# Linear attention with a spatial gating MLP on one core: separate key and query units instead of one unit per head pair

## The chip, the cores and the metric

The kernel runs on one NeuronCore of a Trainium2 chip, in one launch. The metric is the device time of a run in microseconds, as the median of repeated runs. A profile of one execution shows what each engine did: PE is TensorE, ACT is ScalarE, DVE is VectorE, POOL is GpSimd, SP is the engine that only issues DMAs here.

## The reference

Batch 8, 8 heads, 576 tokens, head size 64, 128 features. What is computed, cut to what matters:

```python
def phi(x):
    proj = einsum('bhsd,df->bhsf', x, w_phi)
    proj = proj - max(abs(proj), axis=-1, keepdims=True)
    return concatenate([exp(proj), exp(-proj)], axis=-1)      # 256 features
q_p, k_p = phi(q), phi(k)
kv = einsum('bhsf,bhsd->bhfd', k_p, v);  z = sum(k_p, axis=2)
attn = einsum('bhsf,bhfd->bhsd', q_p, kv) / (einsum('bhsf,bhf->bhs', q_p, z)[..., None] + 1e-06)

x = attn of a batch as (576 tokens, 512)                      # all heads of a token side by side
h = maximum(x @ w_in, 0);  u, v = halves of h                 # 512 columns each
v_n = (v - mean(v)) / sqrt(var(v) + 1e-06)                    # over the 512 columns
v_s = einsum('ts,bsd->btd', w_spatial, v_n) + b_spatial[None, :, None]
out = (u * v_s) @ w_out
```

So `kv` and `z` of a batch need all 576 keys of that batch, a query only needs `kv`; the second half (called B here) needs all heads of a token for `u` and `v`, and all tokens of a batch for the spatial product.

## The kernel before, in words

A batch's 576 tokens are cut into 512 main tokens, four blocks (`NB`) of 128, and 64 tail tokens. The tails of two batches (a group `g`) share one tile of 128 rows.

**Units.** The attention half (A) is cut into 36 units. A main unit is a head pair `pj` of a batch `b`, and holds the keys *and* the queries of all 512 tokens of two heads; a tail unit holds keys and queries of all heads of the two tails of a group. Each unit passes through stages, each in a function:

- `a_transpose` puts k and q with the head dimension on the partitions: with PE and a copy in the first two batches, afterwards `cross` has done it with a DMA transpose on SP's queue (`kT_b`, `qT_b`).
- `a_keys` multiplies by `w_phi` (`by_token`, L232, a 128x256 matmul each, two heads at once with a block-diagonal `wphi2`), takes the largest absolute value on DVE (L244, `mk`) and the two exponentials on ACT (L247, `kf`). `a_scale` scales v by exp of that maximum on POOL (L272, `vs`); the tail's is `tail_scale` (`vst`).
- `a_queries` does the same up to the maximum (L258, `mq`), which POOL splits into a high and a low part (`mhl`); `a_max_t` transposes that on PE (`mT`).
- `a_qfeat` forms the projections with features on the partitions (L304) and subtracts the maxima by one more matmul per head (L308, with `sel`), then two exponentials on ACT (L321, `qf`).
- `a_kv` sums over the keys (L334, L336 for the tail's keys). `a_num` multiplies `qf` by `kv` (L354) and divides in `norm` on DVE (`x`). `a_x_t` transposes `x` to `xT`: on PE with a DVE copy for the first nine units and the last four, otherwise by a DMA transpose on SP's queue (L363).

**The B half.** Its work is a list of tasks of some 0.85 us of matmuls each: `b_v` (L403; then Relu on ACT, statistics on DVE), `b_ln` (POOL: four small operations in `root`, then `normalize`, which writes `vn`), `b_u` (L456), `b_s` (the spatial product, L477 with four `vn` blocks and L478 with the tail's `vnt`; then times `u` on DVE), `b_o` (L500, a copy on ACT, a store on SP), and their tail versions. `b_tasks(b)` gives all tasks of a batch in one go when the last head pair's `xT` has been issued, since a token of `xT` is complete only then. For an odd batch the order is tail `v`, four `v`, `b_ln`, four `u`, tail `u`, the spatial tasks of the even batch, those of the odd batch, then the outputs of both. Batches 0 and 1 (`SPLIT`) are each finished alone.

**The order.** `step(i)` writes down, for each stage in `ORDER`, the unit that is due (`LAGS`: sums two steps after the keys, attention three, out four), and after each stage `fill(share)` takes tasks off the front of the B queue as far as a credit allows, which grows by `RATE` times share, at most to `CAP`. The queue is first in, first out. Loads are put at fixed steps ahead of their unit (`AT`, `AB`, `XP`): k, q and their tails and all weights on POOL's queue, with a cast to bf16 on the way; v, the stores and the DMA transposes on SP's. A tile framework then places semaphores and may move an instruction past others that are not pinned to program order. [...]

Of the kernel before, what the change touches and what calls it, by code (L numbers as in the profile page):

```python
# [11 lines left out]
ALU = mybir.AluOpType  # L12
# [4 lines left out]
def kernel(  # L17
# [29 lines left out]
    POS = [0, 2, 1, 3]  # L47
# [28 lines left out]
    def alloc(b):  # L76
        st[b] = dict(
            q=ld.tile([P, H, NB * D], BF16, tag="q_bf", name="q_bf", bufs=2),
            k=ld.tile([P, H, NB * D], BF16, tag="k_bf", name="k_bf", bufs=2),
            v=ld.tile([P, H * NB, D], FP32, tag="v_f", name="v_f"),  # L80
        )

    def alloc_tail(g):
        gs[g] = dict(
            q=ld.tile([P, H, D], BF16, tag="q_tl", name="q_tl", bufs=1),
            k=ld.tile([P, H, D], BF16, tag="k_tl", name="k_tl", bufs=1),
            v=ld.tile([P, H, D], FP32, tag="v_tl", name="v_tl", bufs=1),
        )

    def load(x, b, h0=0, n=H):  # L90
        if b not in st:
            alloc(b)
        pin(nc.gpsimd.dma_start)(out=st[b][x][:, h0:h0 + n], in_=main_ap(q if x == "q" else k, b, h0, n))

    def load_v(b, eng):
        pin(eng.dma_start)(out=st[b]["v"].rearrange("p (h c) d -> p h (c d)", h=H), in_=main_ap(v, b))

    def load_tail(x, g):
        if g not in gs:
            alloc_tail(g)  # L100
        t, eng = dict(q=(q, nc.gpsimd), k=(k, nc.gpsimd), v=(v, nc.sync))[x]
        for i in range(2):
            pin(eng.dma_start)(out=gs[g][x][i * TL:(i + 1) * TL], in_=tail_ap(t, 2 * g + i))

    def cross(b):
        d = st[b]
        for x in ("k", "q"):
            d[x + "T"] = ld.tile([P, 2 * H, P], BF16, tag=x + "T_b", name=x + "T_b", bufs=2)
            pin(nc.sync.dma_start_transpose)(out=d[x + "T"], in_=d[x].rearrange("p h x -> p (h x)"))


    wphi_f = cpool.tile([P, F], FP32)
    for i in range(2):
        nc.scalar.dma_start(out=wphi_f[i * D:(i + 1) * D, :], in_=w_phi)
    alloc(0)
    first = {}
    for x, t in (("k", k), ("q", q)):
        first[x] = s2.tile([P, 2, NB * D], FP32, tag="ob", name="first", bufs=4)
        pin(nc.sync.dma_start)(out=first[x], in_=main_ap(t, 0, 0, 2))
    ident = cpool.tile([P, P], BF16)  # L120
    make_identity(nc, ident)
    zero = cpool.tile([P, 1], BF16)
    pin(nc.vector.memset)(zero, 0.0)
    wphi2 = cpool.tile([P, 2 * F], BF16)
    pin(nc.vector.memset)(wphi2, 0.0)
    neghalf = cpool.tile([P, NB + 1], FP32)
    pin(nc.vector.memset)(neghalf, -0.5)

    w_spT = cpool.tile([P, NB + 2, S], BF16)
    pin(nc.vector.memset)(w_spT[:, NB:NB + 2, :], 0.0)  # L130
# [3 lines left out]
    for i in range(NM):  # L134
        for tiles, name in ((mhl, "mhl"), (mT, "mT")):
# [6 lines left out]
    pin(nc.vector.tensor_tensor)(out=sel1, in0=ident[:, 0:H], in1=ident[:, H:2 * H], op=ALU.add)  # L142
    pin(nc.vector.tensor_scalar)(out=sel, in0=sel1.unsqueeze(2).to_broadcast([P, H, F]), scalar1=-1.0,
                                 scalar2=None, op0=ALU.mult)
    for x in ("k", "q"):
        pin(nc.vector.tensor_copy)(out=st[0][x][:, 0:2], in_=first[x])
    vst, vnt = [], []
    for i in range(2):
        t = cpool.tile([P, 2, 2, H, DA], BF16, name=f"vst{i}")
        pin(nc.scalar.copy)(out=t.rearrange("p b s h d -> p (b s h d)"), in_=zero.to_broadcast([P, 4 * H * DA]))  # L150
        vst.append(t)
        if i == 0:
            for y in range(2):
                r = slice(y * D, (y + 1) * D)
                pin(nc.scalar.copy)(out=wphi2[r, y * F:(y + 1) * F], in_=wphi_f[r, :])
        t = cpool.tile([P, 2, HALF], BF16, name=f"vnt{i}")
        for bl, row in ((0, TL), (1, 0)):
            pin(nc.scalar.copy)(out=t[:, bl, :], in_=ident[:, row:row + 1].to_broadcast([P, HALF]))
        vnt.append(t)
    load_v(0, nc.sync)  # L160
    for x in ("k", "q", "v"):
        load_tail(x, 0)
    load("k", 0, 2, 2)
    load("q", 0, 2, 2)
    load("k", 0, 4, 4)
    load("q", 0, 4, 4)

# [6 lines left out]
    nc.sync.dma_start(out=bsp_row[TL:TL + 1, :], in_=moe_b_spatial)  # L174
    nc.sync.dma_start(out=bsp_row[0:1, :], in_=moe_b_spatial)
# [9 lines left out]
    EK = 7  # L185
    def transpose_spatial(i):

        pt = psum.tile([P, S], BF16, tag="bank", name="pt")
        if i < NB:
            sc = POS[i]  # L190
            for tp, c in enumerate(POS):
                nc.tensor.transpose(out=pt[:, tp * P:(tp + 1) * P], in_=wsp[:, c, bass.ds(sc, P, step=NB)],
                                    identity=ident)
            nc.tensor.transpose(out=pt[:, T0:S], in_=wspt[:, bass.ds(sc, P, step=NB)],
                                identity=ident[:TL, :TL])
            nc.vector.tensor_copy(out=w_spT[:, i, :], in_=pt)
            return
        for bl in range(2):
            lo = bl * TL
            for tp, c in enumerate(POS):  # L200
                nc.tensor.transpose(out=pt[lo:lo + TL, tp * P:(tp + 1) * P], in_=wspr[:, c, :], identity=ident)
            nc.tensor.transpose(out=pt[lo:lo + TL, T0:S], in_=wspt[:, T0:S], identity=ident[:TL, :TL])
            nc.vector.tensor_copy(out=w_spT[lo:lo + TL, NB + bl, :], in_=pt[lo:lo + TL, :])
        for bl, row in ((0, TL), (1, 0)):
            r = slice(row, row + 1)
            pin(nc.scalar.copy)(
                out=w_spT[r, NB + bl, 0:T0].rearrange("o (a b p) -> o a b p", a=2, b=2),
                in_=bsp_row[r, 0:T0].rearrange("o (p b a) -> o a b p", a=2, b=2))
# [3 lines left out]
    def a_transpose(u):  # L212
        src = st[u["b"]] if u["pair"] else gs[u["g"]]
        if "kT" in src:
            for x in ("kT", "qT"):
                u[x] = src[x][:, 4 * u["pj"]:4 * u["pj"] + 4, :] if u["pair"] else src[x]
            return
        for x, copy in (("k", nc.vector.tensor_copy if u["i"] < EK else nc.scalar.copy), ("q", nc.vector.tensor_copy)):
            pt = psum.tile([P, 4, P], BF16, tag="bank", name="pt")
            for j in range(4):  # L220
                if u["pair"]:
                    blk = src[x][:, 2 * u["pj"] + j // 2, (j % 2) * P:(j % 2 + 1) * P]
                else:
                    blk = src[x][:, 2 * j:2 * j + 2, :]
                nc.tensor.transpose(out=pt[:, j, :], in_=blk, identity=ident)
            u[x + "T"] = a1.tile([P, 4, P], BF16, tag=x + "T", name=x + "T", bufs=2 if x == "k" else 4)
            copy(out=u[x + "T"], in_=pt)
# [7 lines left out]

    def a_keys(u):

        u["mk"] = small.tile([P, H], FP32, tag="mk", name="mk")
        u["kf"] = feat.tile([P, 2, H, F], BF16, tag="kf" if u["pair"] else "kf_t", name="kf",
                            bufs=4 if u["pair"] else 2)  # L240
        for half in range(2):
# [4 lines left out]
            for s, sc in ((0, 1.0), (1, -1.0)):  # L246
                nc.scalar.activation(out=u["kf"][:, s, hs, :], in_=pk, func=AF.Exp, bias=0.0, scale=sc)  # L247

    def a_queries(u):

        m, early = mhl[u["i"] % NM], u["i"] < EARLY
        if not early:
            mq = small.tile([P, H], FP32, tag="mq", name="mq")
        for half in range(2):
            pq = by_token(u["qT"], half)
            if early and half == 0:
                mq = pq[:, 0, 0:H]
            nc.vector.tensor_reduce(out=mq[:, 4 * half:4 * half + 4], in_=pq, axis=AX.X, op=ALU.max,  # L258
                                    apply_absolute_value=True)
        eng = nc.vector if early else nc.gpsimd  # L260
# [3 lines left out]
    def a_scale(u):  # L264
        em = small.tile([P, 2, H], FP32, tag="em" if u["pair"] else "em_t", name="em", bufs=3 if u["pair"] else 1)
        for s, sc in ((0, -1.0), (1, 1.0)):
            nc.scalar.activation(out=em[:, s, :], in_=u["mk"], func=AF.Exp, bias=0.0, scale=sc)  # L267
        if u["pair"]:
            pj = u["pj"]
            vs = feat.tile([P, 2, H, DA], BF16, tag="vs", name="vs", bufs=4)  # L270
# [5 lines left out]
        else:  # L276
            d = gs[u["g"]]
            d["vs"], d["unit"], d["em"] = vst[u["g"] % 2], u, em
            for bl in range(2 if u["i"] > 1 else 1):
                tail_scale(u["g"], bl)  # L280
# [15 lines left out]
    def a_qfeat(u):  # L296
# [3 lines left out]
        for half in range(2):  # L300
            pq = psum.tile([P, 4, P], FP32, tag="bank", name="pq")
            if u["pair"]:
                for par in range(2):
                    nc.tensor.matmul(out=pq[:, 2 * par:2 * par + 2, :], lhsT=wphi2[:, par * F:(par + 1) * F],  # L304
                                     rhs=u["qT"][:, 2 * half:2 * half + 2, :], start=True, stop=False)
                    for x in range(2):
                        j = 4 * half + 2 * x + par
                        nc.tensor.matmul(out=pq[:, 2 * par + x, :], lhsT=sel[:, j, :], rhs=m,  # L308
                                         start=False, stop=(x == 1))
            else:  # L310
                for x in range(4):
                    h = 4 * half + x
                    nc.tensor.matmul(out=pq[:, x, :], lhsT=wphi2[:, (h % 2) * F:(h % 2 + 1) * F],
                                     rhs=u["qT"][:, h // 2, :], start=True, stop=False)
# [369 lines left out]
```

## Time and profile before

| what | value |
|---|---|
| median of 3 runs | 291.54 us (287.78 to 293.93) |
| span of the profiled execution, first to last instruction | 286.4 us |
| PE busy | 261.6 us, 91% |
| ACT busy | 229.3 us, 80% |
| DVE busy | 201.8 us, 70% |
| POOL busy | 182.2 us, 64% |
| moved by DMA | 40.31 MB, mean 141 GB/s |

The page gives no time of its own for the profiled execution but the span; the runs lie 1.4 to 7.5 us above it. In a row of busy tenths each digit is a fortieth of the span, 7.2 us here. In a timeline a line is a start, a duration, an engine, a source line, an operation, what is written and read, and a count; several instructions of one kind that overlap are one line, and in brackets stands the idle time before them and what ended it. In the sums by stretch each engine has its busy time and, in brackets, its count of instructions, in the order PE, PE's weight loads, DVE, ACT, POOL; then come PE's clock, the DMA share and GB/s.

### The profile page before, as it was taken

How to read it: one execution, taken by the hardware profiler on the slowest of the kernel's cores; microseconds unless marked ns; L12 is line 12 of the kernel's file. 1: busy time of each engine (PE TensorE's matmuls, PEld its weight loads, DVE VectorE, ACT ScalarE, POOL GpSimd, SP SyncE). 2: the span in 40 equal slices, each digit the busy share in tenths (PEclk: the TensorE clock that was granted, in tenths of full speed). 3: DMA queues.
4: the chain of work that ended last, by engine and by line, in shares of the span. 5: the costliest groups of instructions: out<-in, count | busy, mean ns of one | idle time of the engine just before them, and what ended most of it. 6: DMA issues, size and time to landing. Idle time of an engine off the chain costs nothing.

```text
span 286.4 us, 7965 instructions
## 1 busy us (share of the span) xinstructions
PE 261.6 (91%) x3070; PEld 178.6 (62%) x3070; DVE 201.8 (70%) x509; ACT 229.3 (80%) x517; POOL 182.2 (64%) x320
## 2 busy tenths in 40 slices
PE   1378889999999999999989999999999999999983
PEld 1157776777666776767557687666667676545441
DVE  4389997977958877598696887578688864354610
ACT  4949998899799988999998679799999746566033
POOL 8159998798336899479689954835969600058200
PEclk9999999999999999999999999999999999999999
DMA  6989999976568499999955994999111003500037
GB/s 185 203 171 120 206 219 223 163 203 71 79 147 186 102 187 155 173 245 196 130 94 102 225 191 87 264 287 255 32 22 32 7 2 122 211 3 0 0 90 242
DMA packets 81706, 40.31 MB, mean 141 GB/s; under 512 B 50242, under 2 KB 77058, under 8 KB 81668
## 3 DMA queue, kind: packets, MB, share of 16 engines
q1 hardware_dynamic: 54180, 28.32, 43.0%
q0 software_dynamic: 27328, 11.41, 35.5%
q8 instruction: 24, 0.39, 0.6%
q14 instruction: 14, 0.11, 0.2%
q10 hardware_dynamic: 160, 0.07, 0.1%
HBM read 32.85 MB, written 9.44 MB: 148 GB/s over the span
## 4 chain that ended last, share of the span: by engine, by line
PE 61%; ACT 14%; DVE 11%; DMA 9%; POOL 2%; issue 2%; ACTq 0%; SPq 0%; POOLq 0%; DVEq 0%
PE pv L403 10%; PE ps L477 8%; PE po L500 7%; PE pu L456 7%; PE ps L232 5%; ACT qf L321 5%; ACT kf L247 5%; PE pv L334 4%; DMA q_tl<-in_q_dram 4%; PE pn L354 4%; DMA out_dram<-ob 3%; PE pq L308 3%; PE pq L304 3%; DVE mk L244 3%; PE ps L478 2%; DVE mq L258 2%
## 5 line engine op out<-in xcount | busy, mean ns | idle before, releaser
L247 ACT ACTIVATE kf<-ps 128x512 bf16<-128x512 f32 x144 | 77.7, 692 | 5.6 <-DVE mk L244 5.4
L272 POOL TENSOR_TENSOR vs<-v_f,em 128x512 bf16<-128x512 f32 x64 | 65.6, 1049 | 23.6 <-ACT em L267 22.6
L321 ACT ACTIVATE qf<-pq 128x512 bf16<-128x512 f32 x128 | 68.2, 675 | 8.5 <-PE pq L308 8.5
L244 DVE TENSOR_REDUCE mk<-ps 128x4 f32<-128x512 f32 x72 | 46.1, 677 | 2.5 <-PE ps L232 2.0
L258 DVE TENSOR_REDUCE mq<-ps 128x4 f32<-128x512 f32 x62 | 39.9, 681 | 4.2 <-PE ps L232 3.4
L502 ACT COPY ob<-po 128x512 f32<-128x512 f32 (+1 forms) x37 | 21.6, 610 | 19.9 <-PE po L500 16.2
L406 DVE BATCH_NORM_STATS2 stats<-vr 128x6 f32<-128x512 bf16 (+1 forms) x37 | 24.8, 687 | 15.8 <-ACT vr L405 15.7
L477 PE MATMUL ps<-w_spT,vn 128*128 128x512 bf16 x128 | 32.8, 379 | 0.0
L456 PE MATMUL pu<-xT,w_in_bf 128*128 128x512 bf16 x128 | 31.6, 379 | 0.0
L403 PE MATMUL pv<-w_in_bf,xT 128*128 128x512 bf16 x128 | 31.2, 379 | 0.0
L480 DVE TENSOR_TENSOR uT<-ps,uT 128x512 bf16<-128x512 f32 x32 | 22.0, 689 | 12.7 <-PE ps L478 11.5
L500 PE MATMUL po<-w_out_bf,uT 128*128 128x512 bf16 x128 | 30.4, 379 | 0.0
L308 PE MATMUL pq<-mT,sel 128*128 128x128 bf16 x256 | 30.0, 219 | 0.0
L308 PEld LDWEIGHTS <-sel 128*128 128x128 bf16 x256 | 25.1, 98 | 3.9
L405 ACT ACTIVATE vr<-pv 128x512 bf16<-128x512 f32 (+1 forms) x37 | 23.3, 691 | 4.0 <-PE pv L403 3.9
L354 PEld LDWEIGHTS <-qf 128*128 128x128 bf16 x512 | 20.4, 97 | 8.2 <-issue 1.7
L345 DVE TENSOR_TENSOR x<-pn,rc 128x256 bf16<-128x256 f32 x64 | 25.0, 418 | 0.5
L420 POOL TENSOR_SCALAR vn<-vr,rs 128x512 bf16<-128x512 bf16 x32 | 24.3, 773 | 0.8
L334 PE MATMUL pv<-vs,kf 128*128 128x66 bf16 x512 | 24.5, 194 | 0.2 <-ACT kf L247 0.2
L354 PE MATMUL pn<-kv,qf 128*128 128x66 bf16 x512 | 22.3, 193 | 1.3 <-ACT qf L321 1.2
L334 PEld LDWEIGHTS <-kf 128*128 128x128 bf16 x512 | 21.7, 97 | 1.8 <-issue 0.9
L304 PE MATMUL pq<-qT_b,wphi 128*128 128x256 bf16 x96 | 22.4, 273 | 0.0
(120 smaller groups left out, 530.8 us busy)
## 6 DMA issues: line engine op xcount, KB each, us to landing
v_f<-in_v_dram SPq DMA_DIRECT2D x8, 1024.0 KB, 10.7
out_dram<-ob SPq DMA_DIRECT2D x32, 256.0 KB, 3.6
k_bf<-in_k_dram POOLq DMA_DIRECT2D x7, 512.0 KB, 7.0
q_bf<-in_q_dram POOLq DMA_DIRECT2D x7, 512.0 KB, 8.7
v_tl<-in_v_dram SPq DMA_DIRECT2D x8, 128.0 KB, 7.7
w_in_bf<-in_moe_w_in_dram POOLq DMA_DIRECT2D x2, 512.0 KB, 8.7
out_dram<-ob SPq DMA_DIRECT2D x8, 128.0 KB, 2.4
k_tl<-in_k_dram POOLq DMA_DIRECT2D x8, 64.0 KB, 6.8
```

The lines of the kernel that those rows point to most:

```text
L244: nc.vector.tensor_reduce(out=u["mk"][:, hs], in_=pk, axis=AX.X, op=ALU.max, apply_absolute_value=True)
L247: nc.scalar.activation(out=u["kf"][:, s, hs, :], in_=pk, func=AF.Exp, bias=0.0, scale=sc)
L258: nc.vector.tensor_reduce(out=mq[:, 4 * half:4 * half + 4], in_=pq, axis=AX.X, op=ALU.max, apply_absolute_value=True)
L272: nc.gpsimd.tensor_tensor(out=vs[:, s, :, 0:D], in0=st[u["b"]]["v"][:, pj * H:(pj + 1) * H, :], in1=em[:, s, :].unsqueeze(2).to_broadcast( ...
L308: nc.tensor.matmul(out=pq[:, 2 * par + x, :], lhsT=sel[:, j, :], rhs=m, start=False, stop=(x == 1))
L321: nc.scalar.activation(out=qf[:, s], in_=pq, func=AF.Exp, bias=0.0, scale=sc)
L334: nc.tensor.matmul(out=pv[:, hh, s, :], lhsT=u["kf"][:, s, 4 * hh + c, :], rhs=u["vs"][:, s, 4 * hh + c, :], start=(c == 0), stop=False)
L354: nc.tensor.matmul(out=pn[:, pos, :], lhsT=u["qf"][hh][:, s, pos, :], rhs=d["kv"][:, 2 * u["pj"] + hh, s, :], start=(s == 0), stop=(s == 1))
L403: nc.tensor.matmul(out=pv[r], lhsT=lhs(kc), rhs=w_in_bf[:, kc, HALF:DFF], start=(kc == 0), stop=(kc == KC - 1))
L456: nc.tensor.matmul(out=pu, lhsT=w_in_bf[:, kc, dc * P:(dc + 1) * P], rhs=d["xT"][:, kc, :], start=(kc == 0), stop=(kc == KC - 1))
L477: nc.tensor.matmul(out=ps, lhsT=d["vn"][:, sp, cs], rhs=w_spT[:, sp, 0:T0], start=(sp == 0), stop=False)
L500: nc.tensor.matmul(out=po[r], lhsT=lhs(dc), rhs=w_out_bf[:, dc, :], start=(dc == 0), stop=(dc == KC - 1))
```

## The change

Keys and queries become units of their own. A key unit is a head pair of a batch as before, without queries; a query unit is a block `c` of 128 tokens with all eight heads. Tails are key units and query units too. Since a query unit holds all heads of its tokens, its `x` and `xT` are complete by themselves: `a_x_t` issues one DMA transpose per block, and `add_tasks` puts the block's `b_v` into the B queue at once; the rest of the batch follows at the last block. Five key units (batch 0 and the tail of group 0) lead, then query units and key units alternate, so the keys of a batch run beside the queries of the batch before. There are 72 half-sized units, so the rate of B tasks per step falls from 3.12 to 1.9, and the credit shares are spread evenly.

Smaller parts: by-token projections of queries are eight 128x128 matmuls a unit (`q_by_token`), the projection with features on the partitions is one 128x512 matmul per half (`a_qfeat`); `u` of batch 0 is made block by block (`u_block`); blocks are no longer held in the order 0, 2, 1, 3 (`POS`); the tail is never split by batch; fills of `vst` and `vnt` move from ACT to DVE and into the loop; `w_phi` is loaded by POOL's queue straight into `wphi2` with a cast; the first q is no longer loaded through SP; `q` of batch 0 comes in one load behind the k loads. `kf`, `vs`, `qf` and `kv` get one more buffer or so. PE transposes of `x` are left for query units 0 to 8 and the last two.

```diff
+    first = s2.tile([P, 2, NB * D], FP32, tag="ob", name="first", bufs=4)
+    pin(nc.sync.dma_start)(out=first, in_=main_ap(k, 0, 0, 2))
...
+    for i in range(2):
+        pin(nc.gpsimd.dma_start)(out=wphi2[i * D:(i + 1) * D, i * F:(i + 1) * F], in_=w_phi)
+    load_v(0)
+    load("k", 0, 2, 2)
+    load("k", 0, 4, 4)
+    load_tail("k", 0)
+    load_tail("v", 0)
+    load("q", 0)
+    load_tail("q", 0)
...
     def a_x_t(u):
+        if u["main"]:
+            d = st[u["b"]]
+            if u["c"] == 0:
+                d["xT"] = s2.tile([P, NB, KC, P], BF16, tag="xT", name="xT", bufs=3)
+            dst = d["xT"][:, u["c"]]
+            if XX <= u["i"] < NQ - 2:
+                nc.sync.dma_start_transpose(out=dst, in_=u["x"].rearrange("p h d -> p (h d)"))
+                return
...
+    ks, qs = [], []
     for g in range(G):
-        if g > 0:
-            units.append(dict(pair=False, g=g, i=len(units)))
...
+        pair = k_main(2 * g) + k_main(2 * g + 1)
+        ks += pair[:NP] + [tail_unit("k", g)] + pair[NP:] if g == 0 else [tail_unit("k", g)] + pair
+        qs += q_main(2 * g) + [tail_unit("q", g)] + q_main(2 * g + 1)
...
+    LEAD = 5
+    units = ks[:LEAD]
+    for i in range(NQ):
+        units.append(qs[i])
+        if i + LEAD < len(ks):
+            units.append(ks[i + LEAD])
...
+        u["step"] = dict(next=i - 1, keys=i, sums=i + 2) if u["kind"] == "k" else dict(
+            next=i - 1, queries=i, maxima=i + 1, features=i + 2, attention=i + 3, out=i + 4)
...
+    def add_tasks(u):
+        g = u["g"]
+        if not u["main"]:
+            queue.append((MM, lambda: b_v_tail(g)))
+            queue.append((MM, lambda: b_u_tail(g)))
+            add_spatial(2 * g)
+            return
+        b, c = u["b"], u["c"]
+        queue.append((MM, lambda: b_v(b, c)))
...
+        if c < NB - 1:
+            return
+        queue.append((0.0, lambda: b_ln(b)))
...
+            queue.extend((MM, lambda dc=dc: b_u(b, dc)) for dc in range(KC))
+        if b % 2 == 1:
+            queue.extend((MS, lambda dc=dc: b_s(b, dc)) for dc in range(KC))
+            queue.append((MS, lambda: b_s_tail(g)))
+            queue.append((MM, lambda: b_o_tail(g)))
+            queue.extend((MM, lambda j=j: b_o(b, j)) for j in range(NB))
...
-    ORDER = (("keys", 0.375), ("queries", 0.25), ("attention", 0), ("sums", 0.25),
-             ("next", 0.125), ("features", 0), ("out", 0), ("maxima", 0))
-    RATE = 3.12
+    ORDER = (("keys", 0.2), ("queries", 0.2), ("features", 0.2), ("attention", 0.2), ("sums", 0.2),
+             ("next", 0), ("out", 0), ("maxima", 0))
+    RATE = 1.9
     CAP = 2.11
```

## The prediction, made before the changed kernel was run

> **What bounds the kernel now.** I read, in this order, the busy rows of the page, the sums by stretch, the timeline for the price of each matmul width, and the tile view of `xT`. The busy rows first:
>
> ```profile
> PE 261.6 (91%) x3070; PEld 178.6 (62%) x3070; DVE 201.8 (70%) x509; ACT 229.3 (80%) x517; POOL 182.2 (64%) x320
> ...
> PE   1378889999999999999989999999999999999983
> PEld 1157776777666776767557687666667676545441
> DVE  4389997977958877598696887578688864354610
> ```
>
> PE is the engine that is nearly always busy, except in the first eight slices (57 us), where DVE shows nines instead. The sums by stretch (0 to 60, 60 to 270, 270 to the end) put numbers on that:
>
> ```profile
> 0.00:60.00 60.00, 43.88 (x546) 33.33 (x547) 47.69 (x136) 48.06 (x106) 46.73 (x78) 1.00 1.17 187
> 60.00:270.00 210.00, 206.59 (x2442) 139.76 (x2441) 151.36 (x369) 175.92 (x404) 135.44 (x243) 1.00 0.71 127
> 270.00:287.00 17.00, 11.18 (x86) 5.49 (x84) 2.76 (x4) 5.27 (x9) 0.00 (x0) 0.99 0.43 140
> ```
>
> The first busy column is PE. From 60 to 270 us it idles 3.4 us of 210; at the end 5.2 (286.4 - 270 - 11.2). A busy PE need not be one that streams, so I price the streams from the timeline:
>
> ```profile
> 38.17 0.66 PE L354 MATMUL pn<-kv,qf 128*128 128x66 bf16 x16 [0.16 <-ACT qf L321]
> 41.24 0.60 PE L232 MATMUL ps<-wphi,kT 128*128 128x256 bf16 x4
> ...
> 262.38 1.06 PE L468 MATMUL pu<-xTt,w_in_bf 128*128 128x128 bf16 x16
> 274.97 7.07 PE L500 MATMUL po<-w_out_bf,uT 128*128 128x512 bf16 x32
> ```
>
> Less one matmul's own duration (0.19, 0.27, 0.22, 0.38 us, from the groups) and divided by the count less one: 0.032, 0.109, 0.056 and 0.216 us for widths 66, 256, 128, 512; width 64 I take at 0.029. The program has 584 matmuls of 512, 416 of 256, 584 of 128, 1280 of 66, 206 of 64: 126.1 + 45.3 + 32.7 + 41.0 + 6.0 = 251.1 us. The span is 286.4, so 35.3 us is lost: 3.4 in the middle, 5.2 at the end, hence 26.7 in the first 60 us. The kernel is a PE stream that is full after the start; only the start offers anything large.
>
> **What the Trainium skill says.** "TensorE: Matmul & The Clock Gate", section "Step-by-step: what each phase is for": matmuls stay in program order, only weight loads are pulled ahead. So one matmul that waits stops all PE work behind it. The trace agrees: PE's gap of 3.35 us before the `k_tl` transposes (12.9 us) is followed by nothing from other streams. The same page's section "The HAM clock gate" has a half-rate clock when PE is sparse: four 256-wide matmuls take 1.06 us at 18.8 us and 0.60 at 23.7, so this start pays it although the clock row reads 9. [...] The tile view of `xT` shows the spread:
>
> ```profile
> DMA to landing us min/median/max: 2.4/3.9/7.7
> ```
>
> **The change, part by part.**
>
> *Matmul work.* The new order has 624 of 512, 176 of 256, 884 of 128, 1280 of 66, 166 of 64: 134.8 + 19.2 + 49.5 + 41.0 + 4.8 = 249.3 us. By-token queries become 128 wide (256 of them), feature projections become 512 wide, batch 0's `u` becomes 128 wide. Gain 1.8 us. ACT loses 18 instructions (fills, `kT` copies), POOL 3, DVE gains one: same loads, ACT still some 205 us if a 512-wide eviction is 0.48 (four `qf` from 23.20 to the next `kf` at 25.13), below PE. Buffers only grow.
>
> *Start.* Key work of batch 0 goes first, with five key units before a query. Loads are reordered: `w_phi` now goes through POOL's queue, then k, k tail, q, q tail, with v on SP. The bytes up to the last of them are the same, and before they landed by 22.0 us; I expect q at about 22. Five key units need DVE 5 x 1.5 and ACT 5 x 2.1 = 10.6 us, so they cannot fill the time up to 22; no B work exists then. k of batch 1 is issued on POOL behind two `vs` groups (2.3 us each) that wait for v (before: landed 12.4, now sharing with k, perhaps 14), so issued near 19 to 20; 7 us to landing gives about 27, against 28.4 before. Its four PE transposes stand between the `sums` of batch 0, so all PE waits there. From then to the first spatial matmul DVE owns the rate. Work there: five key units at 1.5 and one at 1.2, five query units at 3.0 (two reductions 1.2, `qB` 0.33 to 0.66, norms 0.86, small copies), two more half done at 1.9, B work 6.3, `kv` 1.4, the fills that moved from ACT and from before the loop 2.5: 38 us. First spatial matmul at 27 + 38 = 65 at full DVE, 67 with a 5% loss; the order has 37.4 us of matmul work ahead of it, so the start loses about 29.6 against 26.7: +3. Bounds: -4 (q and k land 5 us earlier, DVE still limits) to +9.
>
> *Middle: the `xT` transposes lose their cover.* Before, tasks of a batch were queued in one go behind a long queue; `v` came long after the last DMA transpose. Now each block's `v` is queued as it is out, at a rate of 1.9 a step, and followed step by step in the code that queue is empty, or nearly, at the last block of batches 2 to 6. There `v` follows its own transpose in the same step. Between the end of that block's attention matmuls and its `v` the order leaves 3.7 us of matmuls in five places (last block of 2, 4, 6; third block of 3 and 5) and 2.0 in two (last block of 3 and 5). The way from attention to `xT`: drain and norms 0.8, DVE queue 0.5, transpose 3.9 (median): 5.2 us. PE stands 1.5 us in five places and 3.2 in two: 14 us. Bounds from 2.4 to 7.7 us per DMA: 2 and 38. What waits behind `v`: all PE, then ACT and DVE with it.
>
> *Middle: normalisation loses its cover.* The chain of batch 7's LN in the timeline:
>
> ```profile
> 259.18 0.60 ACT L405 ACTIVATE vr<-pv 128x512 bf16<-128x512 f32 x1 [0.27 <-PE pv L403]
> ...
> 260.53 0.18 DVE L407 BATCH_NORM_AGGREGATE mv<-stats 128x2 f32<-128x6 f32 x1
> ...
> 261.87 0.23 POOL L413 TENSOR_SCALAR var<-mv 128x4 f32<-128x4 f32 x1
> ...
> 263.94 3.03 POOL L420 TENSOR_SCALAR vn<-vr,rs 128x512 bf16<-128x512 bf16 x4
> ```
>
> From `vr` to the last `vn` 7.8 us, about 6.5 without POOL's wait. Batch 2g's spatial matmuls used to stand between an odd batch's LN and its use; now they are done earlier. Odd batches 1, 3, 5 have 6.5 to 7.1 us of matmuls between: about 1 us each with queueing, 3 us (0 to 9). The tail's `vnt` is used 4.1 us of matmuls after its `v`, for a chain of 4.6 (`vr`, stats, four small POOL operations, two `vnt`): 0.75 x 4 = 3 us (0 to 8). The 3.4 us of today stay as about 4. Middle: 14 + 3 + 3 + 4 = 24 against 3.4: +20.5.
>
> *End.* After the last attention batch 7 has only 3.5 us of `u` between its `v` and its spatial matmuls; LN needs 6.5: +2.5 (0 to 4). `uTt`, the last copies and the 4.4 us after PE's last matmul stay; five output copies in a row instead of nine are worth under 1 us.
>
> **Sum.** -1.8 + 3 + 20.5 + 2.5 = +24.2 on the profiled execution: 286.4 to 310.6 us of span. The page gives this execution's span alone; the runs are 287.8 to 293.9, so the median lies 5.1 above it. I carry the difference: 291.5 + 24 = 315.7, said as 315.
>
> **Rivals.**
> - *The stalls are hidden* (no change). If the query side makes up its time, because PE waits let DVE and ACT run ahead and the transposes land near 2.4 us, the middle costs 5 instead of 24: -1.8 + 3 + 1.6 + 2.5 = +5, near 296, or 291 if the start is neutral. For it: ACT and DVE have 17% and 28% to spare in the middle, and SP is quieter in places. Against: matmuls do not pass each other, and no other B work is queued at those points.
> - *An earlier B start* (the other side: faster). Blocks of batch 0 give B work one by one: the first `v` stands after 12.9 us of matmuls, so it would come at about 37 us instead of 47. If this fills PE while DVE keeps up, the start loses 26.7 - 10 = 17; with the middle at 6 and the end as now: 249.3 + 17 + 6 + 6 = 278 span, 283 us. It decides if q is landed before 18 us and DVE loses nothing. Against: DVE has 38 us of work there whatever the order of PE.
> - *Transposes at their slow end.* `xT` shares SP with `kT_b`/`qT_b` (3 us of issue each) and the 1 MB v loads. At 6 us each the seven places cost 28 instead of 14, and gaps over 3 us may halve the clock for a while: about 332.
>
> **How the numbers follow.** My forecast (300 to 325) has 0.60, the slow end 0.18, hidden stalls 0.10 (of it 0.02 over the bound of slower), the early start 0.12. Hence faster 0.12, same 0.08, slower 0.80; 2% is about what a measurement of this kernel can tell from no change. The range 292 to 336 leaves out the faster case and the top of the slow one.
>
> **What would show it.** Right: in the profile after, PE waits at `pv` for the DMA of `xT` in five to seven places, longest 3 to 5 us; PE waits at the spatial matmuls for POOL's `vn` and `vnt`; PE busy falls below 88% with nines broken about every 60 us; DVE nines to 65 us; the first spatial matmul at 65 to 68. Wrong: no wait of PE on `xT`, a first spatial matmul before 58, or PE idle under 6 us from 70 to 270.

## The result: 349 us in place of 293, and the profile after

The changed kernel takes 349.22 us (median of four runs, 347.28 to 351.45), the kernel before 292.74 (287.78 to 294.34). Over fast runs alone, those within 1.5% of the fastest of their kernel, the ratio is 1.208, 95% interval 1.197 to 1.218; the two medians give 1.193. Slower was right; 315 was far too little. The profiled execution has a span of 348.2 us against 286.4, so 61.8 us have to be found. The medians are only 56.5 apart: the profiled execution of the kernel before was one of its quickest (some 288.2 us, an estimate from the 1.8 us that the other runs lie above their spans), so about 5 of the 61.8 us are chance.

The busy rows of the page after, a fortieth being 8.7 us:

```profile
PE 273.3 (78%) x3088; PEld 179.7 (52%) x3130; DVE 210.3 (60%) x510; ACT 224.6 (65%) x501; POOL 180.7 (52%) x317
...
PE   0657687877978897497967999396986999989874
...
DVE  2768687766676767264654585455664686756330
...
PEclk9999899999999999698996999789899999999999
```

PE is nowhere full for long; its two deepest dips in the middle (4 and 3) fall on slices in which the clock row reads 6 and 7. DVE, the engine that was to own the start, shows no nine at all. The sums by stretch (0 to 60, 60 to 330, 330 to the end):

```profile
0.00:60.00 60.00, 36.12 (x443) 27.82 (x447) 40.54 (x103) 33.68 (x79) 38.14 (x57) 0.97 1.00 166
60.00:330.00 270.00, 226.92 (x2571) 146.82 (x2605) 166.29 (x403) 187.84 (x417) 139.51 (x256) 0.95 0.59 108
330.00:349.00 19.00, 10.22 (x78) 5.03 (x80) 3.46 (x5) 3.09 (x6) 3.09 (x5) 0.99 0.21 69
```

PE idles 43 us of the middle 270, where it idled 3.4 of 210, at a mean clock of 0.95; in the first 60 us it does 7.8 us less than before. What PE waits for from 76 to 330 us (us in total, times, longest):

```profile
PE pv L395 <- DMA xT<-x: 21.1, 7, 6.3
PE ps L474 <- POOL vnt L412: 8.2, 4, 2.7
PE po L495 <- DVE uTt L490: 1.7, 3, 0.6
PE pq L332 <- DVE mT L312: 1.4, 2, 0.9
PE ps L473 <- POOL vn L412: 1.1, 3, 0.5
```

Seven waits for the DMA of `xT`, as counted ahead, but 21.1 us and not 14. The tile view says that a typical transpose was quicker than before, with a long tail:

```profile
DMA to landing us min/median/max: 2.4/2.4/8.6
```

The longest wait, in the timeline (norm of the block on DVE, transpose on SP, last matmuls before the wait and the `v` after it on PE):

```profile
134.62 0.42 DVE L360 TENSOR_TENSOR x<-pn,rc 128x256 bf16<-128x256 f32 x1
...
135.41 1.73 SPq L382 DMA_TRANSPOSE xT<-x  x1
...
137.42 0.39 PE L332 MATMUL pq<-mT,sel 128*128 128x128 bf16 x4
144.06 1.89 PE L395 MATMUL pv<-w_in_bf,xT 128*128 128x512 bf16 x4 [6.25 <-DMA xT<-x]
```

The transpose was issued 0.4 us after its `x` was done and landed at 144.0, 8.6 us later. An output store issued at 134.05 landed at 143.5, and a `kT_b` transpose issued at 129.88, ahead of both on SP's queue, took until 140.7, so other transfers were slow there too. The second longest wait (5.34 us, up to 225.8) is alike: a transpose of 8.0 us, issued 5.2 us after a `kT_b` transpose. That the `kT_b` transposes are the cause was not tested. With no other task in the queue, all of PE stood.

Then there is the clock. Behind a wait of 2.2 us at 158.9 to 161.15 us it is at half for one stretch (157 to 161, 161 to 165, 165 to 169; the number after POOL's is the clock):

```profile
157.00:161.00 4.00, 1.87 (x18) 1.11 (x17) 2.18 (x5) 1.61 (x4) 3.55 (x8) 1.00 0.61 117
161.00:165.00 4.00, 3.85 (x16) 1.96 (x17) 1.34 (x3) 1.08 (x2) 1.25 (x4) 0.57 0.99 182
165.00:169.00 4.00, 3.95 (x52) 2.46 (x52) 3.47 (x10) 2.63 (x7) 1.10 (x2) 1.00 0.01 2
```

PE is busy in the second stretch and its matmuls take twice as long: 512-wide ones are spaced 0.43 us and not 0.216. The trace has seven such stretches, six after 130 us, of 3.4 or 6.8 us each.

**Where the 61.8 us are.** I count, for each kernel, the matmuls begun by 76 us, each at the spacing that the prediction took from the timeline. The kernel before has 50.4 us of stream by then, this one 35.9: a start loss of 25.6 against 40.1 us. What is then left of the span beyond its stream is 286.4 - 251.1 - 25.6 = 9.7 and 348.2 - 249.3 - 40.1 = 58.8 us. So the stream gives -1.8, the start +14.5, the rest +49.1. In the rest are 21.1 us for `xT`, 12.3 for `vn` and `vnt` (the whole run: 4.1 and 8.2), 10.7 that matmuls took longer in the six half-clock stretches after 76 us, 4.7 after the last matmul, and, as what is left, some 10 in short waits. The rest of the kernel before is 4.4 after the last matmul and 5.3 of such waits. (42 matmul records are missing in this trace, so a wait may read 0.2 us too long; where they are missing before 76 us, in this and in other runs, a start loss reads up to about 1 us too high.)

### The profile page after: what moved, and what is told of

The parts are those of the page before. It is cut to its first block, busy times and chain, and to the rows that moved or that the text cites. A ratio compares the mean times of both kernels' runs of the same rounds, so it can differ in the third digit from the quotient of the medians.

```text
span 348.2 us, 8016 instructions
## 1 busy us (share of the span) xinstructions
PE 273.3 (78%) x3088; PEld 179.7 (52%) x3130; DVE 210.3 (60%) x510; ACT 224.6 (65%) x501; POOL 180.7 (52%) x317
## 4 chain that ended last, share of the span: by engine, by line
PE 39%; POOL 16%; DVE 16%; DMA 12%; ACT 10%; issue 5%; POOLq 0%; SPq 0%; ACTq 0%; DVEq 0%
DMA xT<-x 9%; PE ps L473 7%; PE po L495 6%; PE pv L395 6%; POOL vn L412 5%; POOL vs L290 4%; DVE mk L264 4%; ACT kf L267 4%; DVE stats L398 3%; ACT qf L336 3%; PE ps L242 3%; POOL rs L406 2%; PE ps L474 2%; PE pn L371 2%; PE pq L332 2%
## 5 line engine op out<-in xcount | busy, mean ns | idle before, releaser
L336 ACT ACTIVATE qf<-pq 128x512 bf16<-128x512 f32 x144 | 74.5, 605 | 21.7 <-PE pq L332 21.7
L395 PE MATMUL pv<-w_in_bf,xT 128*128 128x512 bf16 x115 | 33.7, 404 | 27.1 <-DMA xT<-x 21.1
L276 DVE TENSOR_REDUCE mq<-ps 128x4 f32<-128x512 f32 x72 | 46.4, 679 | 10.8 <-PE ps L252 5.8
L398 DVE BATCH_NORM_STATS2 stats<-vr 128x6 f32<-128x512 bf16 x36 | 24.6, 685 | 25.1 <-ACT vr L397 25.0
L397 ACT ACTIVATE vr<-pv 128x512 bf16<-128x512 f32 x36 | 21.8, 611 | 26.9 <-PE pv L395 26.2
L497 ACT COPY ob<-po 128x512 f32<-128x512 f32 x36 | 20.8, 614 | 18.0 <-PE po L495 17.0
L395 PEld LDWEIGHTS <-xT 128*128 128x128 bf16 x128 | 11.2, 100 | 37.9 <-DMA xT<-x 21.8
L360 DVE TENSOR_TENSOR x<-pn,rc 128x256 bf16<-128x256 f32 x72 | 28.8, 421 | 1.1
L448 PE MATMUL pu<-xT,w_in_bf 128*128 128x512 bf16 x112 | 29.2, 398 | 0.0
L332 PEld LDWEIGHTS <-sel 128*128 128x128 bf16 x288 | 22.1, 100 | 9.8 <-issue 3.5
L371 PEld LDWEIGHTS <-qf 128*128 128x128 bf16 (+1 forms) x640 | 23.3, 101 | 6.5 <-issue 0.9
L371 PE MATMUL pn<-kv,qf 128*128 128x66 bf16 (+1 forms) x640 | 24.9, 195 | 0.0
```

What stands on the lines that cost most here:

```text
L332: nc.tensor.matmul(out=pq[:, x, :], lhsT=sel[:, 4 * half + x, :], rhs=m, start=False, stop=(x == 3), skip_group_check=True)
L336: nc.scalar.activation(out=qf[:, s], in_=pq, func=AF.Exp, bias=0.0, scale=sc)
L371: nc.tensor.matmul(out=pn[r, y, :], lhsT=u["qf"][half][:, s, y, r], rhs=st[b]["kv"][:, 4 * half + y, s, :], start=(s == 0), stop=(s == 1))
L395: nc.tensor.matmul(out=pv[r], lhsT=lhs(kc), rhs=w_in_bf[:, kc, HALF:DFF], start=(kc == 0), stop=(kc == KC - 1))
```

## The experiments

Unless said otherwise each kernel has one timed execution, beside the kernel before on the same chip (288.9 to 293.1 us). Repeated runs of one kernel lie 2 us, at times 5, from their median, so differences under 4 us are not read, and one of 5 between two single runs only together with what the traces show. The table has the two losses as just defined; "rest" is span - stream - start loss, with 249.3 us of stream for every variant of the changed kernel (so the rest of e3 contains 4.9 us of added PE transposes).

| kernel | us | span | clock | start loss | rest |
|---|---|---|---|---|---|
| before | 292.7 | 286.4 | 1.00 | 25.6 | 9.7 |
| after | 349.2 | 348.2 | 0.956 | 40.1 | 58.8 |
| e1_wait2: after, tasks two steps later | 330.4 | 328.6 | 0.960 | 39.8 | 39.5 |
| e2_rate156: after, rate 1.56 | 326.9 | 325.2 | 0.984 | 40.0 | 35.9 |
| e3_pe_xt: after, all `xT` on PE | 332.6 | 330.9 | 0.995 | 40.4 | 41.2 |
| e4_ahead: after, PE transposes earlier | 350.1 | 348.3 | 0.951 | 41.2 | 57.8 |
| e6_lead6: after, six keys ahead | 370.2 | 368.4 | 0.931 | 40.6 | 78.5 |
| e14_lags_only: after, all lags doubled | 335.3 | 333.5 | 0.969 | 37.1 | 47.1 |
| e5_order: e2 + spatial order of before | 319.5 | 317.7 | 0.984 | 39.2 | 29.2 |
| e7_all: e5 + six keys ahead | 327.5 | 325.7 | 0.973 | 40.1 | 36.3 |
| e9_lags: e5 + some lags doubled | 320.0 | 318.3 | 0.984 | 42.6 | 26.4 |
| e10_hold0: e5 + batch 0's tasks at once | 314.5 | 312.7 | 0.991 | 36.5 | 26.9 |
| e11_lags_hold0: e9 + e10 | 313.4 | 311.7 | 0.983 | 39.9 | 22.5 |
| e12_all_late: e11 + the other lags | 303.4 | 301.6 | 0.989 | 38.0 | 14.3 |
| e13_dve_light: e12 + less DVE work | 297.7 | 295.9 | 0.988 | 32.7 | 13.9 |
| e15_best: e13 + `w_phi`, sums later | 297.7 | 295.4 | 0.988 | 33.0 | 13.1 |
| e16_early5: e15 + `EARLY` back | 297.3 | 297.2 | 0.985 | 34.7 | 13.2 |
| e8_before_rate: before, rate 4.2 | 307.3 | 305.5 | 0.989 | 27.2 | 27.2 |

### The transposes: three ways to take the wait away

In e1 a block's tasks enter the queue two steps after its `x` is out:

```diff
-            ... attention=i + 3, out=i + 4)
+            ... attention=i + 3, out=i + 4, tasks=i + 4 + WAIT)     # WAIT = 2, stage "tasks" runs add_tasks
```

> The changed kernel with one edit: a block's B tasks are queued two steps after its x has been handed to the transpose, not in the same step. Theory 1 (the v matmuls follow their own DMA transpose and stop PE for 21.1 us, and the pauses then halve PE's clock for another 8 to 10 us): the wait of pv on xT falls below 4 us and the span from 348 to 318-325. Theory 2 (the query and key units are half as large, so every step is a chain of short dependent pieces, and PE waits for this chain wherever the B tasks stand): the wait on xT goes but turns up elsewhere, span 340 or more. Theory 3 (the start alone is what is late): unchanged within 5 us after 76 us.

In e2 the rate goes to half of the 3.12 that a full unit had; in e3 (`XX = 99`) every `x` is transposed on PE.

```diff
-    RATE = 1.9
+    RATE = 1.56
```

> The changed kernel with RATE 1.56 in place of 1.9, half of the 3.12 per full-size step before, so that the B queue is not run empty at the last block of batches 2 to 6; the tasks left over run after the attention half. Theory 1: the waits on xT fall below 5 us, first spatial matmul as in the changed kernel at 76, span 318-326. Theory 2: fewer B matmuls per step leave PE waiting for the chain of the attention half in the middle, span 345 or more, with waits on mT, qf and kT instead of xT.

> The changed kernel with XX = 99: all transposes of x on PE with a DVE copy, no DMA transpose of x. It adds 22 x 4 transposes of 0.056 us, 4.9 us of PE, and 22 copies of 0.42 us on DVE. Theory 1: a v then follows a copy, which cost 0.8 to 1.5 us a place at the start of the changed kernel, instead of 2.4 to 6.4 us of DMA: waits 21 to about 8, less time at half clock, span 328-338. Theory 2: no gain, span 348-355.

330.4, 326.9 and 332.6 us: all three give 17 to 22 us of the 56. The expected ranges are spans: 325.2 and 330.9 us of e2 and e3 lie in those of theory 1, 328.6 of e1 lies 3.6 above; none comes near the 340 and more of theory 2. So theory 1 holds for a good third of the loss and leaves the rest open. In e1 and e2 the waits of PE after 76 us begin with other names (e2's list ends at 300 us; by the end of the run its `vn` has grown to 5.5):

```profile
PE ps L474 <- POOL vnt L412: 8.8, 4, 3.2
PE pv L395 <- DMA xT<-x: 4.7, 4, 2.0
...
PE ps L474 <- POOL vnt L412: 7.1, 3, 3.0
PE ps L473 <- POOL vn L412: 3.2, 5, 1.5
```

The first two lines are e1's, the others e2's, which has no wait for the DMA left. In e1 a transpose still took up to 13.2 us: what went is the standing behind it. In e3 the clock stays full in the middle, and the copy behind each PE transpose takes 6.9 us of waits instead.

### The start: transposes earlier, one more key unit

```diff
-        u["step"] = dict(next=i - 1, keys=i, ...
+        nx = i - (2 if i >= AHEAD else 1)                           # AHEAD = 7
+        u["step"] = dict(next=nx, keys=i, ...                       # the same for query units
```

> The changed kernel with the transposes of k and q on PE (first two batches and tails) written two steps ahead of their use rather than one, from the eighth unit on. Theory 3 (the start is slow because PE stands between its own transposes and their DVE copies, 5 to 6 us between 27 and 76 us): first spatial matmul from 76.4 to 70-72, span 341-344. If DVE sets the rate of the start, as the prediction had it: first spatial matmul unchanged within 2 us, span 346-350.

350.1 us (span 348.3): nothing, as in the second case; over the whole run waits for `kT` went down by 2.8 us and those for the copy of `xT` up by 2.0.

In the timeline of after, PE stands at the batch's sums for the tail's scaled v, with the next key unit behind it, and ACT is empty until that unit's keys have come:

```profile
22.95 2.06 POOL L305 TENSOR_TENSOR vst<-v_tl,em 64x512 bf16<-64x512 f32 x2
...
25.26 0.21 PE L351 MATMUL pv<-vst,kf 128*128 128x66 bf16 x1 [1.95 <-POOL vst L307]
...
28.77 1.09 ACT L267 ACTIVATE kf<-ps 128x512 bf16<-128x512 f32 x2 [6.70 <-DVE mk L264]
```

e6 has `LEAD = 6` in place of 5, one key unit more to fill this hole.

> The changed kernel with six key units ahead of the first query in place of five, rate unchanged at 1.9. Theory H (ACT's empty 6.7 us at 22 to 28.8 us is the start's loss: PE stands in program order at the sums, waiting for the tail's scaled v from POOL, with the next key unit behind it): the sixth key unit fills it, the first spatial matmul comes at 71-73 us instead of 76.4, the run takes 343-346 us against 349. Rival theory C (after 29 us the pairs of one key and one query unit run at 8 us each whatever leads them, as their chain PE-DVE-ACT-PE is longer than the work of any engine): the hole only moves, first spatial matmul at 75-78 and the run within 3 us of 349.

370.2 us, and a start loss unchanged at 40.6. Both theories of the start say at most 3 us more; the 21 us came in the middle:

```profile
PE pv L395 <- DMA xT<-x: 29.2, 7, 9.0
PE ps L474 <- POOL vnt L412: 9.2, 4, 3.3
```

Beside the 8 us more for `xT`, a wait of 5.2 us for output copies (`ob`) is new, and matmuls take some 18 us longer at half clock where it was 10.7. `LEAD` shifts all key units, with the loads and transposes tied to them, by one place against the queries. Which transfers then meet was not followed; so why a single unit more costs 21 us stays open.

### The spatial order, the lead again, and the kernel before with a drained queue

e5 keeps the rate of 1.56 and restores the place of the spatial tasks:

```diff
-            add_spatial(2 * g)                      # with the tail unit
...
-            queue.extend(... b_s(b, dc) ...)        # odd batch: its own s, st, ot, its own o
+            for x in (b - 1, b): queue.extend(... b_s(x, dc) ...)   # then st, ot, and o of both
```

> The changed kernel with the rate 1.56 and, in addition, the queue order of the kernel before: spatial tasks of both batches of a group only after the odd batch's u, and the group's tail unit queues only its v and u. Theory O (the spatial tasks stand too close behind the normalisations of vn and vnt on POOL, because the even batch's spatial work is queued with the tail): waits of PE for vn and vnt, 8.8 + 3.5 us in the changed kernel and 7.1 + 5.5 with the rate alone, fall to 4 us or less, and the time from 327 to 315-320. Rival theory P (POOL itself is late in the middle, wherever the spatial tasks stand): the waits stay over 8 us in sum and the time stays at 324-330.

319.5 us, 7.4 less than e2. No wait for `vn` or `vnt` is left (e2 had 12.6 us of them), theory O holds; the waits that head the list now are of another kind:

```profile
PE pt L311 <- POOL mhl L280: 4.6, 4, 1.8
PE pv L395 <- ACT qf L336: 2.4, 3, 0.9
```

e7 is e5 with `LEAD = 6`.

> The three together: rate 1.56, six key units ahead, spatial order as before. If the gains add (22 us of the rate, 8 to 12 of the order, 4 of the lead): 308-315 us, middle waits of PE under 12 us, what is left over the kernel before being the start. If the order and the lead give nothing: 324-330. Slower than the kernel before (290) in both cases.

327.5 us: the lead costs 8 us here too, again none of it gained in the start. The number falls in the second range, but not for its reason: the order had given 7 us and the lead took 8.

e8 is the kernel before with nothing changed but `RATE = 4.2`.

> The kernel before, its units unsplit, with one number changed: tasks are taken off the queue at a rate of 4.2 a step in place of 3.12, so that the queue is empty at the end of each batch and v follows its last transpose in the same step. Theory Q (a drained queue is what costs in the middle, with or without the split into key and query units): slower by 8 us or more, 298-312 us, with PE waiting for xT. Rival theory U (the split units are what costs, a drained queue harms only with them): within 4 us of 290.

307.3 us: theory Q. The unsplit kernel loses 18 us against the 288.85 on the same chip, 15 against the median of 292.7, as soon as its queue drains. The rest grows from 9.7 to 27.2, with one wait for `xT` and more than a dozen short ones:

```profile
PE pv L403 <- DMA xT<-x: 3.9, 1, 3.9
```

So a backlog of tasks is a good part of the cover that made the middle of the kernel before full, whatever the units. That the shape of the units costs nothing doesn't follow: e2, whose slower rate keeps a backlog, still has 35.9 us of rest.

### The lags: a part of them does nothing

e10 puts batch 0's tasks into the queue in one go, at its last block. e9 doubles the lags of five stages (sums; maxima, features, attention, out); e11 has both.

```diff
-        u["step"] = dict(next=i - 1, keys=i, sums=i + 2) ...
-            next=i - 1, queries=i, maxima=i + 1, features=i + 2, attention=i + 3, out=i + 4)
+        u["step"] = dict(next=i - 1, keys=i, sums=i + 4) ...
+            next=i - 1, queries=i, maxima=i + 2, features=i + 4, attention=i + 6, out=i + 8)
```

> The kernel of the rate 1.56 and the spatial order of before (319.5 us), with the lags of the stages doubled in steps: sums four steps after the keys; maxima, features, attention and out of a query two, four, six and eight steps after its by-token matmuls in place of one to four. A step is half a unit of the kernel before, so this restores the lag in time that its stages had. Theory L (halved units with lags still counted in steps leave each chain PE-DVE-POOL-PE and PE-ACT-PE half the cover; this is what makes the many small waits, about 17 us of them from 30 to 76 us and some 15 us for mhl, qf, mT, x later): 300-308 us. Rival theory M (the small waits come from where the queue's tasks stand, or from DVE and ACT being late, not from the lags): 316-323.

> The same kernel of 319.5 us with the tasks of batch 0 put into the queue in one go when its last block is out, as before, and not block by block. Theory B (in the start, tasks of the second half set between the units make PE stand behind fresh xT copies and delay the by-token matmuls that feed DVE and ACT): the rows of DVE and ACT before 50 us fill up, the start loses 5-10 us less, 310-315 us. Rival theory L (the lags set the pace of the start): the start runs no faster, the tasks only come later: 319-325.

> Both of the last two edits. If theories L and B both hold and add: 295-303 us; if only L: as with the lags alone within 3 us; if neither: 316-325. Under 290 in no case, since the start's data and DVE work remain.

320.0, 314.5 and 313.4 us. e10 is 5 us faster, in theory B's range, though only 2.7 of them are start loss, where 5 to 10 were expected. The doubled lags give nothing, 0.5 us slower in e9 and 1.1 faster in e11, which fits no case of e11's expectation: after 76 us the waits of e9 for `mhl` and `qf` are nearly gone, and those for the copy of `xT` are 6.7 us where e5 had 0.9. Read alone, this would have killed theory L. But two links were as short as in the changed kernel, the tasks in the same step as the transpose of `x` and the PE transposes one step before their matmuls, and in e11 these lead the list from 25 us on (`kT` 7.1, `xT` 5.3, `qB` 5.1 us). e12 moves them (the edits of e1 and e4 on top of e11).

> The kernel of 313.4 us (rate 1.56, spatial order and batch 0's tasks as before, doubled lags), with the two links that the doubled lags left at one step also given two or more: tasks are queued two steps after x is out, and the PE transposes of k and q stand two steps ahead of their matmuls. Left in that kernel are 12 us of waits of PE for kT, qB and qT and 6 to 8 us for xT. Theory L2 (each short chain needs two of the half steps, and shifting only some of them moves the wait to the others): 302-308 us. Rival theory M2 (PE gets ahead of DVE whatever the order, the waits only change their name): 311-316.

303.4 us, 10 less, in the range of L2, and the rest falls from 22.5 to 14.3. The list after 76 us begins with:

```profile
PE po L495 <- DVE uTt L490: 2.3, 3, 0.8
PE pv L395 <- ACT qf L336: 1.0, 2, 0.6
```

So in e9 and e11 the waits moved to the links that had stayed short, and moving these two gains 10 us. That the doubled lags are needed for this gain, as L2 says, is not shown: no run moves the two links on the kernel of e10 without doubling the lags.

Are the lags the whole story then? e14 puts the doubled lags of all stages into the changed kernel and leaves its rate, spatial order and batch 0 alone.

> The changed kernel (rate 1.9, spatial order and batch 0's tasks as the change has them) with one thing altered: all lags between dependent stages doubled in steps, tasks queued two steps after x is out, PE transposes two steps ahead. Theory T (all the loss in the middle is lags that the halved step cut in half; the drained queue, the spatial order and the split only show it): 305-315 us, with waits for xT gone. Rival theory S (several causes add, and the lags are the last 10 to 16 us of them): 325-338, since PE still runs out of tasks at the ends of batches.

335.3 us: theory S. But e1, which moves the tasks alone, took 330.4: the doubled lags and the earlier transposes add nothing to its gain here. The wait for the DMA of `xT` shrinks to a seventh, but the normalisations take its place (up to 300 us; by the end of the run 13.5 and 9.8):

```profile
PE ps L474 <- POOL vnt L412: 11.7, 3, 5.5
PE ps L473 <- POOL vn L412: 7.1, 7, 2.6
PE pv L395 <- DMA xT<-x: 3.1, 1, 3.1
```

Alone, all the lags are worth 14 us, moving the tasks 19, the rate 22; the order gives 7 after the rate. Rate, order, batch 0 and all the lags together make 46 of the 56.

### What is left in the start

e13 is e12 with the fills of `vnt` on ACT (two copies each) and `EARLY = 0`, so that POOL splits all query maxima.

> The kernel of all doubled lags with work taken off DVE in the start: the fills of vnt on ACT in two copies each (as before), and the high and low parts of the query maxima on POOL from the first unit on; together some 6 us of DVE between 27 and 60 us. Theory D (what is left of the start's loss is DVE, full from 30 to 50 us): 4-6 us faster than the same kernel without this. Rival theory C (the chain of each pair sets the start): within 2 us of it.

297.7 us: theory D. From 27 to 50 and from 50 to 76 us, first the changed kernel, then e13 (PE first, DVE third, ACT fourth):

```profile
27.00:50.00 23.00, 16.36 (x238) 13.13 (x238) 18.86 (x49) 14.39 (x34) 13.18 (x18) 0.93 1.30 207
50.00:76.00 26.00, 20.30 (x299) 15.73 (x302) 18.31 (x48) 19.46 (x43) 14.66 (x24) 1.00 0.55 103
...
27.00:50.00 23.00, 18.47 (x292) 15.97 (x290) 20.09 (x49) 18.83 (x48) 19.22 (x35) 0.88 1.33 213
50.00:76.00 26.00, 23.62 (x382) 19.29 (x382) 21.93 (x59) 23.90 (x58) 18.46 (x33) 1.00 0.79 155
```

DVE goes from 37.2 busy us of 49 to 42.0, and ACT from 33.9 to 42.7. In e12 DVE was already at 43.7 with 5.3 us less of stream behind it: once the order lets DVE run, its own work counts. The fills and the splits were moved together, so their shares are not told apart.

e15 brings `w_phi` through ACT's queue, as before, and sets batch 0's sums two steps later; e16 sets `EARLY` back to 5. These two were timed in three rounds.

> The kernel of 297.7 us with the two waits left in its start shortened: w_phi comes through ACT's queue in fp32 and is cast by ACT, as before (3.5 us of PE waiting for it), and batch 0's sums stand two steps later, so that PE does not stand at the tail's scaled v from POOL (2.5 us). If both come off the end: 291-294 us, level with the kernel before; if the start is bound by DVE from 40 to 60 us whatever comes first: 296-299. Under 288 only if DVE and ACT gain the whole time.

> The kernel of 297.7 us (all steps so far, with w_phi through ACT and batch 0's sums two steps later) with one number set back: the high and low parts of the first five query maxima on DVE again, not on POOL. In that kernel PE stands 3.7 us at the first transposed maxima, for mhl behind a full POOL (9.8 of 10 us busy from 30 to 40 us), while DVE is half empty there. Theory P (POOL's queue at 30 to 40 us is the last wait of the start): 293-296 us. Rival theory D (DVE is then full from 40 to 60 us and loses as much): 297-299.

297.74 us (ratio to before 1.019, interval 1.010 to 1.028) and 297.33 (1.019, 1.011 to 1.027): slower than the kernel before, and whether by 2% is unclear. Both lie in the second range of their expectation, the one in which DVE binds. The waits that they aim at go away, and the time does not. In e15 PE stands 3.7 us for `mhl` behind a full POOL, in e16 it meets DVE's `x` and `kT` in place of that (1.7 and 1.6 us), with the splits back on DVE. No kernel here beats the one before. By its profile e15 has 7.4 us more of start loss and 3.4 more of rest, less 1.8 of stream, 9 us against the quick profiled execution of the kernel before; the medians are 4.6 apart. What makes this difference stays open.

## Why the prediction was wrong

The forecast span of 310.6 us is 37.6 short of the 348.2. In the terms of its own sum the start took 10.5 us more than forecast (40.1 of loss, not 29.6), the half clock 10.7 where there is no term, `xT` 7.1 more, the other waits 6.0 more, normalisation and the end 3.3 more. So two steps failed above all: that DVE would run nearly without a pause from 27 us to the first spatial matmul, and that a wait of PE costs no more than its own length. Third comes the price of a wait on `xT`.

- **Stream, -1.8.** It is a count of instructions; nothing measured speaks against it.
- **Start, +3.** It was +14.5. The term of 38 us at a DVE that is full all the time failed. The data was not the limit: q landed at 17.6 us where 22 was expected, k of batch 1 at 22.7 and not 27, and PE waited 0.5 us for it. With that the same sum would have given 61 us for the first spatial matmul at full DVE; it came at 76.5. The amount of work was right, DVE was busy 39.0 us from 22.7 to 76.4; but that is 73% of the time, not 95. The prediction took an engine's sum of work for the time of a stage, in an order where each unit waits for links of other engines. e10 (-2.7 us of start loss, little more than such a figure can tell) points to batch 0's tasks between the units, e13 (-5.3) to DVE's own small work; the rest of it is not settled.
- **`xT`, 14 us.** The seven places were right and the mechanism too. The size was 21.1, inside the bounds of 2 to 38 (which come to 3.4 and 40.5 from the prediction's own figures). With the median as measured (2.4 us, not 3.9) the sum would have given 3.4; two waits of 6.25 and 5.34 us, on transposes of 8.6 and 8.0 us, are over half of the 21.1. A median is the wrong price where waits count only above a cover. Of the kernel before only the spread to 7.7 us showed it.
- **Half clock.** 10.7 us after 76 us, for which the forecast has no term; only the rival of slow transposes names it, for gaps over 3 us. Each of the six stretches follows on a wait for `xT` or `vnt`, kinds that the prediction did see, four of them on one of 2.2 to 2.6 us. e3, without the waits for the DMA, has no half clock between 42 us and its end.
- **Normalisation, 3 + 3 us.** 12.3 us. That the spatial tasks stand too near was right, and e5 shows it (the waits go, -7.4 us); the chain was priced with POOL free, and `vs` of the key units shares it: two of them, 2.0 us from 156.43 on, stand just ahead of the chain that PE waits for until 161.15.
- **Other waits, 4 us.** Some 10. Two things have no line in the sum: the queue that drains takes the cover from every dependent task, not from `xT` alone, and the split halves the time between stages, for lags are counted in steps. e8 shows the first in the old structure. The second is likely but not shown by itself: lags alone gave nothing in e9 and e11, and the 10 us of e12 came with the two links.
- **End, +2.5.** The wait for `vn` there is 2.9 us, and 4.7 us lie after the last matmul: near enough.
- **Adding up.** The causes don't add like terms: e2 removes 21 us of waits for `xT` and 7 of half clock and gains 22, e14 removes 18 us of `xT` and pays 11 of them to `vn` and `vnt`. A term for a wait that goes has to ask which wait stands next.

Of the rivals, the one of slow transposes (332) came nearest, and half in its mechanism: 21 us of waits, and the clock; but the typical transpose was quick, and of the seven that PE waited for only two were as slow as that. The earlier start did not come: q had landed before 18 us, as it asked, but the first `v` stood at 42.3 us, not at 37. Of the signs named, the seven waits, `vn`, `vnt` and PE under 88% came; DVE's nines and a first spatial matmul by 68 us did not.

## What to carry to other kernels

Where an order written by hand counts its lags in steps, a unit half as large halves the time of every link. Look for the link that PE waits at and lengthen that one: doubling the others gave nothing here (e9, e11, and e14 beside e1). A backlog of independent tasks is cover for a PE that takes its matmuls in order; a rate that empties it before the end of a batch cost 22 us in the changed kernel and 15 to 18 in the old one, so price a change by the backlog that stays at each dependent task. Keep waits of PE short for a second reason: the clock that follows.

## What the runs showed of the hardware

The Trainium skill, "TensorE: Matmul & The Clock Gate", section "The HAM clock gate", has the clock fall back after an idle window of about 3.4 us. In these traces less was enough. The seven half-clock stretches of the changed kernel begin at 38.13, 140.54, 161.02, 181.50, 188.32, 222.46 and 242.94 us, all whole multiples of 3.41 us apart, so the clock seems to be set once per window of that length. In the window ahead of each, PE was busy for 0.68 to 1.39 us, 20 to 41%; in every other full-clock window from 35 us to its last matmul for at least 1.61 us, 47%, and there the clock stayed. So waits of 2.2 us (up to 161.15) and 2.6 us (up to 180.25) sufficed, because most of each fell into one window. Over the traces of all 18 kernels here the line is less sharp: every such window with PE busy under 41% was followed by half clock, none over 54%, and between these some were and some not.

A fill of one row cost as much as one of all: in the start DVE wrote two single rows of `vnt` in 1.11 us, and all 128 partitions of it in 0.48 (as 512 words of four bytes a row, where the single rows are 512 of two).

```profile
27.71 0.48 DVE L60 MEMSET vnt<- 128x512 uint32 x1
28.90 1.11 DVE L60 MEMSET vnt<- 1x512 bf16 x2 [0.16 <-DVE mk L264]
```
